# Half-row load for the last filter chunk, other TensorE fillers in the front, and a new instruction order, in a one-core H3 block with a token MLP

## The chip, the core and the metric

The kernel runs on one core of one Trainium2 chip. The metric is the device time of one execution in microseconds (us), the median of the runs that are shown; lower is better.

## The reference, cut to what matters

S = 2048 positions, D = 448 channels, F = 1792 hidden units, one batch, bf16 in and out. LN is a layer norm without weights.

```python
k_shift[s] = sum over t in 0..3 of k_pad[s + t] * shift_k[:, 3 - t]      # short causal convolution
kv = k_shift * v
y  = irfft(rfft(kv padded to 4096) * rfft(ssm_k padded to 4096))[:2048]  # long causal convolution, per channel
h  = x + LN(x) * (y + kv * ssm_D)                                        # x is A_q
z  = LN(LN(h))
out = h + transpose( gelu( z.T @ w1 + b1 ) @ w2 + b2 )                   # the MLP mixes positions, not channels
```

## The kernel before, in words

**Layout.** Position s = 16 q + r lies on partition q, in row r. Everything has 128 partitions and sixteen rows of 448 channels. The long convolution is done as a Fourier transform in two matmul stages, separately for the filter ("k1", "k2") and for kv ("u1", "u2"), then a product and two inverse stages ("i1", "i2"), then the MLP ("mlp").

**Orders written out by hand.** A step of the program is named `tag.n:m`, operation m of step n of tag. `ORDER` (L12) lists for each of the five engines every operation in the order in which that engine runs it. `_Sched.op` records each operation with what it reads and writes; `_Sched.schedule` (L322) replays the five lists to hand out the eight PSUM banks, and `emit` puts a semaphore wait ahead of each operation for what it depends on. So each engine runs its list strictly in order, and an operation that waits holds up everything behind it in its own list. DMAs are issued from the lists of SP and POOL (two from ACT).

**The front (tags dummy, loads, tables, kv, kT, k1, u1).**

- `dummy.0:1-9` (L1025) are nine matmuls of ones, 128x448, whose result nobody reads; they run while the first loads are on their way. The same matmul is used as a filler behind three of the transposing steps: `kT.1:9-11`, `kT.3:9-11`, `kT.5:9-11`, three each.
- `loads.0` to `loads.3` (L887) bring the four chunks of the filter `A_ssm_k` to KN: three of 128 channels and one of 64 channels, 4096 bytes a channel. `loads.6`, `.8`, `.10`, `.5` (L898) bring k, rows 0-3, 4-7, 8-11, 12-15; `loads.7`, `.9`, `.11`, `.12` (L901) bring v likewise. `loads.13:1` (L905) is ssm_D in 16 copies, `loads.14` (L908, L910) the two biases, `loads.4` (L890, L893) the taps.
- `kT.0` to `kT.7` (L1038) turn KN around on TensorE, chunk c and half g of the rows in step 2c + g, eight transposes each. `kT.6` and `kT.7` are the 64-channel chunk: 64x64 transposes.
- `kv.1` to `kv.8` (L966) turn k around, `kv.9` to `kv.16` (L992) are the short convolution, multiplied by v on DVE (L1007) as it leaves PSUM.
- `tables.5` and `tables.6` make the Fourier tables E (DVE L837 to L844, then a sine on ACT, L847); `tables.4` and `tables.7` make the smaller tables of the later stages (POOL, DVE, one sine on ACT, L862).
- `k1.4i+jh` and `u1.4i+jh` (L1059) are the first transform stage: eight matmuls a step, one cast of 128x896 from PSUM (L1069 on ACT or DVE; L1067 on DVE for k1.0 to k1.3), and after each second step three DMAs (two from POOL, one from SP, L1075) that shuffle the partitions. The casts go to a ring of four buffers that is released when these DMAs have landed.

**The middle.** `k2.n` and `u2.n` (L1094) are the second stage, four matmuls a step, whose casts (L738, L739 on ACT; L741, L742 on DVE) can go to either engine. Sixteen DVE products (L1160) follow, the inverse stage `i1` (L1177) with its casts (L738) and its partition shuffle (POOL L1200, SP L1200, and L1189 for the last group), and `ct` (L1108), which turns the tables around. The first product, `i1.0:0`, waits for all shuffles of k1 and u1, as its output lies over their ring. `warm` (L1210) are 14 matmuls that nobody reads. `q` and `xn` are the layer norm of x.

**The end.** `i2` (L1299, L1307) finishes the convolution row by row; for each row DVE (L1336, L1342, L1345, L1374, L1385), ACT (L1316, L1354) and POOL (L1364 to L1378) make the gated sum, its norm and the row Q[r]. `mlp.0` to `mlp.15` (L1432) multiply Q[r] with seven blocks of w1, `mlp.17` to `.23` (L1442) do the other seven, `mlp.24` to `.39` (L1454) are the second matrix with the outputs. w1 comes in eight DMAs (`w1a.0-3`, L1405, `w1b.0:0-3`, L1409), w2 in four (L1416), all from SP. `w1a.0` is needed by mlp.0.

The waits that the change touches stand in these lines:

```python
r=[(o_KN + 4096 * c, 4096), (o_ID, 256)], bw=[b], kind="tr", mode=4 if c == 3 else 0,   # kT
after=shuf["zl"] if h else shuf["u"], safter=(wl[0],) if h else ())                      # w1a.0 after all u1 shuffles
```

Of the kernel before, what the change touches and what calls it, by code (L numbers as in the profile page):

```python
# [13 lines left out]
        "dummy.0:1-9 kv.4:0-11 kv.3:0-7 kv.6:0-11 kv.5:0-7 kT.1:0-7 kT.0:0-3 kT.1:9-11 kT.0:4-7 kT.3:0-7 kT.2:0-3 "  # L14
        "kT.3:9-11 kT.5:0-7 kT.2:4-7 kT.5:9-10 kT.6:0-7 kT.7:0-7 bias.0:0 kT.5:11 kv.7:0-7 kv.2:0-3 k1.12:0-7 "
        "k1.8:0-7 k1.9:0-7 kv.2:4-11 kv.1:0-7 k1.10:0-7 k1.11:0-7 kT.4:0-7 kv.8:0-3 k1.13:0-7 k1.14:0-7 kv.8:4-11 "
        "kv.10:0-23 kv.12:0-23 kv.9:0-27 k1.4:0-7 k1.15:0-7 kv.11:0-27 u1.0:0-7 u1.1:0-7 k1.0:0-7 k1.1:0-7 u1.2:0-7 "
        "u1.3:0-7 kv.13:0-27 u1.4:0-7 k1.5:0-7 kv.14:0-23 k1.6:0-7 u1.6:0-7 u1.5:0-7 k1.2:0-7 kv.15:0-27 k1.7:0-7 "
        "u1.7:0-7 u1.8:0-7 u1.9:0-7 k1.3:0-7 k2.0:0-3 k2.1:0-3 k2.12:0-3 k2.13:0-3 k2.4:0-3 k2.5:0-3 kv.16:0-23 "
        "k2.9:0-3 k2.8:0-3 u1.10:0-7 u1.12:0-7 u1.13:0-7 u1.14:0-7 u1.11:0-7 u1.15:0-7 k2.2:0-3 k2.3:0-3 k2.7:0-3 "  # L20
        "k2.6:0-3 k2.10:0-3 k2.11:0-3 k2.14:0-3 k2.15:0-3 u2.0:0-3 u2.1:0-3 u2.12:0-3 u2.13:0-3 u2.8:0-3 u2.9:0-3 "
        "u2.6:0-3 u2.7:0-3 i1.1:1-7 i1.1:10-17 i1.1:8 i1.14:10-16 i1.14:1-7 i1.14:17 i1.14:8 i1.8:1-7 i1.8:10-16 "
        "i1.8:8 i1.8:17 ct0.0:0-7 u2.10:0-3 u2.11:0-3 i1.10:1 i1.10:10-17 i1.10:2-8 u2.5:0-3 u2.4:0-3 i1.12:1-8 "
        "i1.12:10-17 u2.3:0-3 u2.2:0-3 i1.6:1-8 i1.6:10-17 u2.14:0-3 u2.15:0-3 i1.4:9-15 i1.4:0-6 i1.4:16 i1.4:7 "
        "warm.12:0 warm.13:0 i1.16:1-7 i1.16:10-17 i1.16:8 ct.2:0-7 ct.1:0-7 ct.0:0-7 warm.0:0 warm.1:0 warm.2:0 "
        "warm.3:0 warm.4:0 warm.5:0 warm.6:0 warm.7:0 warm.8:0 warm.9:0 warm.10:0 warm.11:0 i2.1:0-1 i2.2:0-3 "
        "i2.9:0-1 i2.10:0-3 i2.17:0-1 i2.45:0-1 i2.20:0-1 i2.32:0-1 i2.28:0-1 i2.54:0 i2.41:0-1 i2.54:1 mlp.0:2 "
        "mlp.0:4 mlp.0:3 mlp.0:0 i2.58:0-1 mlp.0:6 mlp.0:5 mlp.0:1 mlp.1:6 mlp.1:1 mlp.1:3 mlp.1:5 mlp.1:0 mlp.1:4 "
        "mlp.1:2 i2.67:0-1 mlp.2:4-6 mlp.2:0-3 i2.71:0-1 mlp.3:1 mlp.3:0 mlp.3:5 mlp.3:4 mlp.3:2-3 mlp.3:6 mlp.4:2 "
        "mlp.4:1 mlp.4:6 mlp.4:5 mlp.4:4 mlp.4:0 mlp.4:3 i2.80:0-1 mlp.5:1 mlp.5:5-6 mlp.5:0 mlp.5:2 mlp.5:4 "  # L30
        "mlp.5:3 i2.84:0-1 mlp.6:1 mlp.6:6 mlp.6:0 mlp.6:3 mlp.6:5 mlp.6:4 mlp.6:2 i2.93:0-1 mlp.7:6 mlp.7:3 "
        "mlp.7:0 mlp.7:2 mlp.7:4-5 mlp.7:1 i2.97:0-1 mlp.8:2-3 mlp.8:0 mlp.8:6 mlp.8:4-5 mlp.8:1 mlp.9:0 mlp.9:3-5 "
        "mlp.9:2 mlp.9:6 mlp.9:1 mlp.10:5 mlp.10:4 mlp.10:6 mlp.10:0-1 mlp.10:3 mlp.10:2 mlp.11:3 mlp.11:6 mlp.11:2 "
        "mlp.11:0-1 mlp.11:4-5 mlp.12:2 mlp.12:0-1 mlp.12:3-6 mlp.13:2 mlp.13:1 mlp.13:0 mlp.13:3-6 mlp.14:3 "
        "mlp.14:2 mlp.14:6 mlp.14:1 mlp.14:5 mlp.14:4 mlp.14:0 mlp.15:6 mlp.15:0 mlp.15:2 mlp.15:4 mlp.15:3 "
        "mlp.15:5 mlp.15:1 mlp.17:0-15 mlp.18:0-15 mlp.19:0-15 mlp.20:0-15 mlp.21:0-15 mlp.22:0-15 mlp.23:0-15 "
        "mlp.24:0-13 mlp.25:0-13 mlp.26:0-13 mlp.27:0-13 mlp.28:0-13 mlp.29:0-13 mlp.30:0-13 mlp.31:0-13 "
        "mlp.32:0-13 mlp.33:0-13 mlp.34:0-13 mlp.35:0-13 mlp.36:0-13 mlp.37:0-13 mlp.38:0-13 mlp.39:0-10 "
        "mlp.39:16-17 mlp.39:11 mlp.39:18-20 mlp.39:12 mlp.39:21-22 mlp.39:13 mlp.39:23-29 "
    ),  # L40
    "act": (
        "tables.0:5 kv.4:12 kv.3:8 kv.6:12 tables.6:3 tables.5:3 kT.6:8 tables.7:5 k1.8:8 k1.9:8 k1.10:8 k1.11:8 "
        "k1.13:8 kT.4:8 kv.8:12 k1.15:8 k1.4:8 u1.0:8 u1.1:8 u1.2:8 u1.3:8 u1.4:8 k1.5:8 k1.6:8 u1.5:8 u1.6:8 "
        "k1.7:8 u1.8:8 u1.9:8 k2.1:4 k2.13:4-5 k2.5:5 k2.9:4 u1.12:8 u1.13:8 u1.14:8 u1.15:8 k2.3:5 k2.7:5 k2.11:4 "
        "k2.15:4 u2.1:4 u2.13:4-5 u2.9:4-5 u2.7:4-5 i1.1:18 i1.1:9 i1.14:9 i1.14:18 i1.8:9 i1.8:18 u2.11:4-5 "
        "i1.10:18 i1.10:9 u2.5:4 i1.12:9 i1.12:18 u2.3:5 u2.3:4 i1.6:9 i1.6:18 u2.15:4-5 i1.4:17 i1.4:8 xn.2:0 "
        "i1.16:18 i1.16:9 ct.2:8 xn.1:0 i1.16:21 ct.0:8 ct.1:8 xn.4:0 xn.5:0 i2.46:0 i2.19:0 i2.29:0 i2.22:0 "
        "i2.33:0 i2.42:0 i2.31:0 i2.59:0 i2.35:0 i2.44:0 i2.68:0 i2.48:0 i2.72:0 i2.57:0 i2.61:0 i2.81:0 i2.70:0 "
        "i2.85:0 i2.74:0 i2.83:0 i2.98:0 i2.87:0 i2.96:0 i2.100:0 mlp.16:6 mlp.16:2 mlp.16:0 mlp.16:4 mlp.16:3 "
        "mlp.16:5 mlp.16:1 mlp.17:16 mlp.18:16 mlp.19:16 mlp.20:16 mlp.21:16 mlp.22:16 mlp.23:16 mlp.39:15 "  # L50
    ),
    "dve": (
        "dummy.0:0 tables.3:0-1 kv.0:3 tables.6:0 tables.4:16 tables.5:0 tables.4:17 tables.6:1 tables.4:18 "
        "tables.5:1 tables.4:19 tables.6:2 tables.4:20 tables.5:2 kT.1:8 tables.7:6 kT.0:8 kT.3:8 tables.7:4 "
        "tables.7:7 kv.5:8 kT.5:8 kT.2:8 kT.7:8 bias.0:1 kv.7:8 k1.12:8 kv.2:12 kv.1:8 kv.0:4 k1.14:8 kv.10:24-25 "
        "kv.12:25 kv.12:24 kv.9:28-29 kv.11:29 kv.11:28 k1.0:8 k1.1:8 kv.13:28-29 kv.14:25 kv.14:24 k1.2:8 bias.1:0 "
        "kv.15:29 kv.15:28 u1.7:8 k1.3:8 k2.1:5 k2.5:4 kv.16:24-25 k2.9:5 u1.10:8 u1.11:8 k2.3:4 k2.7:4 k2.11:5 "
        "k2.15:5 u2.1:5 i1.0:0 i1.1:0 i1.14:0 i1.13:0 i1.7:0 i1.8:0 i1.10:0 i1.9:0 ct0.0:8 q.1:0 q.1:2 q.1:1 q.1:3 "
        "i1.11:0 i1.12:0 q.2:0 u2.5:5 i1.5:0 i1.6:0 i1.3:0 i1.2:0 q.3:0 xn.0:1 q.2:2 i1.15:0 i1.16:0 q.3:2 q.3:1 "
        "q.3:3 q.2:3 q.2:1 q.4:0 q.4:2-3 q.4:1 q.5:0 q.5:2 q.5:1 q.5:3 q.6:2 q.6:0 q.6:3 q.6:1 q.7:2 q.7:0 i2.3:0 "  # L60
        "xn.3:1 i2.4:0 i2.11:0 i2.5:0 i2.18:0 i2.6:0 i2.12:0 i2.21:0 i2.13:0 q.7:1 i2.8:0 i2.14:0 i2.55:0 i2.30:0 "
        "i2.16:0 i2.34:0 q.7:3 i2.43:0 i2.26:0 i2.27:0 i2.47:0 q.8:2 q.8:0-1 q.8:3 i2.39:0 i2.56:0 i2.60:0 i2.40:0 "
        "i2.69:0 i2.73:0 i2.52:0 i2.53:0 i2.86:0 i2.94:0 i2.65:0 i2.82:0 i2.95:0 i2.66:0 i2.78:0 i2.99:0 i2.79:0 "
        "i2.92:0 i2.91:0 i2.105:0 i2.104:0 mlp.24:14 mlp.25:14 mlp.26:14 mlp.27:14 mlp.28:14 mlp.29:14 mlp.30:14 "
        "mlp.31:14 mlp.32:14 mlp.33:14 mlp.34:14 mlp.35:14 mlp.36:14 mlp.37:14 mlp.38:14 mlp.39:14 mlp.39:30 "
    ),
    "pool": (
        "tables.4:0 tables.4:2 tables.4:4 tables.4:6 tables.4:8 tables.4:10 tables.4:12 tables.4:14 tables.4:1 "
        "tables.4:3 tables.4:5 tables.4:7 tables.4:9 tables.4:11 tables.4:13 tables.4:15 tables.1:0 tables.0:1-2 "
        "tables.0:0 tables.0:3-4 loads.13:0 tables.2:0-1 tables.2:3 tables.2:5 tables.2:7-11 tables.2:2 tables.2:4 "  # L70
        "tables.2:6 q.0:0-1 kv.0:1-2 tables.7:0-3 tables.7:8-11 kv.0:0 k1.9:9-10 k1.11:9-10 k1.13:9-10 k1.15:9-10 "
        "u1.1:9-10 u1.3:9-10 k1.1:9-10 k1.5:9-10 u1.5:9-10 k1.3:9-10 k1.7:9-10 u1.7:9-10 u1.9:9-10 u1.13:9-10 "
        "u1.15:9-10 u1.11:9-10 ew.0:3 ew.0:1 ew.0:0 i1.14:19 i1.14:21 i1.8:19 i1.8:21 i1.1:19 i1.1:21 ew.0:2 "
        "q.1:4-5 i1.10:19 i1.10:21 xn.0:0 i1.12:19 i1.12:21 i1.6:19 i1.6:21 i1.4:18 i1.4:20 q.2:4-5 q.6:4-5 xn.3:0 "
        "q.4:4-5 i2.7:0 i2.23:0-1 i2.15:0 i2.23:2 i2.24:0 i2.25:0 i2.36:0-2 i2.37:0 i2.49:0 i2.38:0 i2.49:1-2 q.8:4 "
        "i2.50:0 q.8:5 i2.51:0 i2.62:0-2 i2.63:0 i2.64:0 i2.75:0-2 i2.76:0 i2.0:0 i2.77:0 i2.88:0-2 i2.89:0 i2.90:0 "
        "i2.101:0-2 i2.102:0 i2.103:0 "
    ),
    "sp": (
        "loads.6:0 loads.8:0 loads.0:0 loads.1:0 loads.2:0 loads.3:0 loads.13:1 loads.14:0-1 loads.10:0 loads.5:0 "  # L80
        "loads.11:0 loads.4:0-2 loads.12:0 loads.9:0 loads.7:0 k1.9:11 k1.11:11 k1.13:11 k1.15:11 u1.1:11 k1.1:11 "
# [501 lines left out]
def _build(nc, A_q, A_k, A_v, A_shift_k, A_ssm_k, A_ssm_D, B_w1, B_b1, B_w2, B_b2, out):  # L583
# [54 lines left out]
    with ctx:  # L638
# [89 lines left out]
        T_KX = -27.67  # L728
        T_EW = -10.0
        T_CP, T_XL, T_WB = 39.11, -35.53, 156.06  # L730
        N_WZ, N_WI, N_W0, N_WK, N_WJ = 14, 0, 9, 3, 0

        def evac(dst, src, w, b, n, scale=None, engs=FX, r=(), est=None):

# [782 lines left out]
```

## Time and profile before

| what | value |
|---|---|
| median of the runs shown | 173.49 us (173.15 to 173.97) |
| profiled execution, its own time | 173.37 us |
| its span, first to last instruction | 171.6 us |
| around the span | 1.8 us |
| busy in the span | PE 162.5, DVE 100.9, ACT 92.6, POOL 59.4 us |
| granted TensorE clock | 1.00 in every slice |

The profile is of one execution. "Idle before" is the time in which an engine had nothing ready; a group's mean is that of one instruction, and consecutive instructions of one engine overlap by about a tenth of a microsecond, so that sums over a sequence are taken here from start to start. PE stands for matmuls, PEld for the weight loads that run beside them, and the times in the timeline are in us from the first instruction.

### The profile page before, as it was taken

The page shows a single profiled execution, that of the slowest core. Times are in us where ns is not written, and L with a number is a line of the kernel's source. Part 1 is how long each engine was busy: PE and PEld are TensorE (multiplying, and loading weights), DVE is VectorE, ACT ScalarE, POOL GpSimd, SP SyncE. Part 2 cuts the span into 40 slices and gives each one's busy share as a digit, 9 for nine tenths or more (in the row PEclk, how much of TensorE's full clock was granted, in tenths as well). Part 3 has the DMA queues.
Part 4 walks back from the last instruction along what each step waited for, and adds up shares of the span by engine and source line. Part 5 has one row for each costly group of instructions (what it writes and reads, how often), then busy time and mean ns, then how long its engine had stood idle before and what let it go on. Part 6 is the DMA issues. An engine that isn't in the chain of part 4 may idle for free.

```text
span 171.6 us, 3585 instructions
## 1 busy us (share of the span) xinstructions
PE 162.5 (95%) x1431; PEld 94.6 (55%) x1431; DVE 100.9 (59%) x187; ACT 92.6 (54%) x133; POOL 59.4 (35%) x152
## 2 busy tenths in 40 slices
PE   6989999989889999988999999999999999999994
PEld 2776745452324333533455455555567777777783
DVE  7998797879899999979997730000003133132231
ACT  3786978988999999978975816321210000000000
POOL 8345727564810696444898730000000000000000
PEclk9999999999999999999999999999999999999999
DMA  5999757676859776547989999980000111101111
GB/s 160 418 308 384 248 180 273 245 281 208 274 132 408 254 212 177 160 153 219 329 314 392 407 424 419 418 351 11 0 4 0 53 53 53 53 4 53 53 53 54
DMA packets 15628, 35.15 MB, mean 205 GB/s; under 512 B 3740, under 2 KB 9740, under 8 KB 15612
## 3 DMA queue, kind: packets, MB, share of 16 engines
q1 hardware_dynamic: 12468, 28.25, 45.3%
q0 software_dynamic: 2880, 6.49, 12.0%
q8 instruction: 11, 0.18, 0.4%
q10 hardware_dynamic: 264, 0.18, 0.3%
q14 instruction: 5, 0.04, 0.1%
HBM read 22.05 MB, written 1.84 MB: 139 GB/s over the span
## 4 chain that ended last, share of the span: by engine, by line
PE 67%; ACT 17%; DMA 7%; DVE 3%; POOL 2%; issue 2%; DVEq 0%; ACTq 0%
PE ps L1454 25%; ACT arena L738 13%; PE ps L1432 12%; PE ps L1442 12%; DMA arena<-arena 7%; PE ps L1025 3%; PE ps L1059 3%; PE ps L1094 3%; ACT arena L1069 3%; PE ps L966 3%; PE ps L1038 3%; PE ps L1299 2%; PE ps L992 2%; ACT arena L739 2%; POOL arena L1075 2%
## 5 line engine op out<-in xcount | busy, mean ns | idle before, releaser
L1457 DVE SCALAR_TENSOR_TENSOR arena<-ps,arena 128x448 bf16<-128x448 f32 (+2 forms) x17 | 11.1, 656 | 57.2 <-PE ps L1454 57.2
L1454 PE MATMUL ps<-arena 128*128 128x448 bf16 (+2 forms) x238 | 42.7, 342 | 0.0
L1454 PEld LDWEIGHTS ps<-arena 128*128 128x128 bf16 x238 | 33.3, 145 | 9.5
L738 ACT CAST arena<-ps 128x896 bf16<-128x896 f32 x30 | 24.5, 1006 | 0.3 <-PE ps L1094 0.2
L1432 PE MATMUL ps<-arena 128*128 128x448 bf16 x112 | 22.5, 353 | 0.6 <-DVE arena L1374 0.6
L1075 POOL DMA_DIRECT2D arena<-arena x32 | 17.5, 553 | 13.2 <-ACT arena L1069 9.9
L1069 ACT CAST arena<-ps 128x896 bf16<-128x896 f32 x23 | 19.5, 913 | 3.8 <-PE ps L1059 3.5
L1442 PE MATMUL ps<-arena 128*128 128x448 bf16 x112 | 21.4, 352 | 0.0
L1422 ACT ACTIVATE arena<-ps,arena 128x448 bf16<-128x448 f32 x14 | 8.2, 640 | 19.6 <-PE ps L1442 14.7
L1432 PEld LDWEIGHTS ps<-arena 128*128 128x128 bf16 x112 | 10.7, 98 | 11.3 <-DVE arena L1374 1.0
L1094 PE MATMUL ps<-arena 128*64 128x448 bf16 x128 | 15.1, 360 | 1.7 <-ACT arena L739 0.7
L1160 DVE TENSOR_TENSOR arena<-arena 128x1792 bf16<-128x1792 bf16 x16 | 16.6, 1085 | 0.3
L1442 PEld LDWEIGHTS ps<-arena 128*128 128x128 bf16 x112 | 11.0, 98 | 10.2
L1177 PE MATMUL ps<-arena 64*128 64x448 bf16 x128 | 14.7, 351 | 1.1 <-DVE arena L1160 0.7
L1059 PE MATMUL ps<-arena 128*32 128x448 bf16 x256 | 15.2, 355 | 0.5
L1200 POOL DMA_DIRECT2D arena<-arena x14 | 8.3, 596 | 13.2 <-ACT arena L738 13.2
L1094 PEld LDWEIGHTS ps<-arena 128*64 128x64 f16 x128 | 5.7, 108 | 10.3 <-ACT arena L738 3.2
L1177 PEld LDWEIGHTS ps<-arena 64*128 64x128 f16 x128 | 5.9, 94 | 9.7 <-DVE arena L1160 3.2
L738 ACT COPY arena<-ps 128x1024 bf16<-128x1024 bf16 (+2 forms) x9 | 8.3, 977 | 3.3 <-PE ps L966 2.8
L1007 DVE TENSOR_TENSOR arena<-ps,arena 128x512 bf16<-128x512 f32 (+1 forms) x16 | 9.0, 616 | 1.4 <-PE ps L992 1.4
L1354 ACT ACTIVATE arena<-arena 128x448 bf16<-128x448 f32 x14 | 8.0, 573 | 3.0 <-DVE arena L1326 2.9
L1059 PEld LDWEIGHTS ps<-arena 128*32 128x32 f16 x256 | 5.0, 95 | 7.9 <-ACT arena L1069 2.4
(96 smaller groups left out, 195.5 us busy)
## 6 DMA issues: line engine op xcount, KB each, us to landing
arena<-in_B_w_dram SPq DMA_DIRECT2D x8, 896.0 KB, 7.8
arena<-in_B_w_dram SPq DMA_DIRECT2D x2, 2048.0 KB, 17.6
arena<-arena SPq DMA_DIRECT2D x16, 224.0 KB, 3.0
arena<-arena POOLq DMA_DIRECT2D x32, 112.0 KB, 3.5
arena<-in_B_w_dram SPq DMA_DIRECT2D x2, 1536.0 KB, 20.1
arena<-arena POOLq DMA_DIRECT2D x14, 196.0 KB, 4.7
arena<-in_A_k_dram SPq DMA_DIRECT2D x4, 448.0 KB, 5.5
arena<-in_A_v_dram SPq DMA_DIRECT2D x4, 448.0 KB, 8.7
```

The source lines that it names most:

```text
L738: return e.copy(out=dst(), in_=src())
L1007: return e.tensor_tensor(out=v, in0=u.rearrange("p t (r d) -> p t r d", d=64), in1=v, op=ALU.mult)
L1059: op("pe", lambda e, W, b=b, r=r, q=q, x=x, c0=c0: e.matmul(PS[32 * q:32 * q + 32, b.slots[x], 0:D], E[:, 2 * r + x, c0:c0 + 32], src[:, r ...
L1069: return e.copy(out=dst, in_=Ppair(b)) if W == "act" else e.tensor_copy(out=dst, in_=Ppair(b))
L1075: shuf[tag].append(op(q_, lambda e, W, g=g, i=i, a=a, nu=nu, jh=jh: e.dma_start(T[a + i:a + i + 4 * nu - 3:4].rearrange("p (j k) c d -> p ...
L1094: op("pe", lambda e, W, b=bs[h], h=h, j=j, c=c, par=par: e.matmul(PS[64 * par:64 * par + 64, b.slots[c], 0:D], FW[:, 64 * c:64 * c + 64], ...
L1160: op("dve", lambda e, W, m=m, i=i: e.tensor_tensor(out=MR(m.slots[0]).rearrange("p (x y) d -> p x y d", x=2), in0=TU[:, i].unsqueeze(2).br ...
L1177: k = op("pe", lambda e, W, b=bs[h], m=ms[h], par=par, t=t, tab=tab, xy=xy, P=P: e.matmul(Pb(b, par), tab[P, :], MR(m.slots[0])[P, xy, :], ...
L1432: op("pe", lambda e, W, r=r, fc=fc, b=bs[fc]: e.matmul(Pb(b), W1A[:, r, 128 * fc:128 * fc + 128], Q[:, r, :], start=(r == 0), stop=(r == R ...
L1442: op("pe", lambda e, W, r=r, fc=fc, b=b: e.matmul(Pb(b), W1B[:, r, 128 * (fc - n0):128 * (fc - n0) + 128], Q[:, r, :], start=(r == 0), sto ...
L1454: op("pe", lambda e, W, r=r, fc=fc, b=b, d0=d0, d1=d1: e.matmul(Pb(b)[:, d0:d1], W2[fc // 7][:, fc % 7, r:S:R], G[:, fc, d0:d1], start=(fc ...
L1457: op("dve", lambda e, W, r=r, b=b, A=A, d0=d0, d1=d1: e.scalar_tensor_tensor(out=X[:, r, d0:d1], in0=Pb(b)[:, d0:d1], scalar=bm[:, r:r + 1 ...
```

## The change

**Loads and transposes of the last filter chunk.** The 64 channels of 4096 bytes are loaded as 128 half channels of 2048 bytes. `kT.6` and `kT.7` are no longer eight transposes of 64x64 each but sixteen matmuls each: 128 half rows against the even or the odd columns of the identity, 64 columns wide, the two halves into the lower and the upper 64 partitions of one PSUM bank, in f32.

**Fillers.** A new tag `fill` puts five matmuls like the dummies ahead of the nine. Behind the kT steps one filler is left (`kT.1:9`) of nine.

**w1a.0** waits for one inverse shuffle (`i1.8:21`) instead of all u1 shuffles.

**ORDER** is another one on all engines. The parts that the prediction uses are below; in words: on SP k rows 4-7, filter chunks 0 and 2 come first, then k rows 0-3, chunks 3 and 1; ssm_D, the second bias and v rows 8-11 go behind two shuffle issues; w1a.0 goes behind the i1.16 shuffles, and w1a.1 to w1a.3 are spread between the late i1 shuffles. On POOL `tables.7` goes from before the first shuffles to between them. On DVE `tables.5` goes ahead, `tables.4` behind the transposes. ACT no longer copies kv.4 and kv.6.

```diff
 "pe"
-dummy.0:1-9 kv.4:0-11 kv.3:0-7 kv.6:0-11 kv.5:0-7 kT.1:0-7 kT.0:0-3 kT.1:9-11 kT.0:4-7 kT.3:0-7 kT.2:0-3
-kT.3:9-11 kT.5:0-7 kT.2:4-7 kT.5:9-10 kT.6:0-7 kT.7:0-7 bias.0:0 kT.5:11 kv.7:0-7 kv.2:0-3 k1.12:0-7
...
-i2.1:0-1 i2.2:0-3 i2.9:0-1 i2.10:0-3 i2.17:0-1 i2.45:0-1 i2.20:0-1 i2.32:0-1 i2.28:0-1 i2.54:0 i2.41:0-1 i2.54:1 mlp.0:2
-mlp.0:4 mlp.0:3 mlp.0:0 i2.58:0-1 mlp.0:6 mlp.0:5 mlp.0:1 ...
+fill.0:0 fill.2:0 fill.4:0 fill.3:0 fill.1:0 dummy.0:1-9 kv.6:0-3 kv.5:0-7 kT.1:0-7 kT.1:9 kT.0:0-7
+kv.6:4-11 bias.0:0 kT.5:0-7 kv.3:0-6 kv.4:0-11 kT.6:0-15 kT.7:0-15 kv.3:7 kT.3:0-7 kT.2:0-7 kv.7:0-7
+k1.8:0-7 k1.12:0-7 k1.9:0-7 kv.2:0-3 kv.1:0-7 ...
+i2.1:0-1 i2.2:0-3 i2.9:0-1 i2.10:0-3 i2.45:0-1 i2.32:0-1 i2.17:0-1 i2.20:0-1
+i2.28:0-1 warm.0:0 i2.54:0-1 i2.41:0-1 i2.58:0-1 mlp.0:3 mlp.0:6 mlp.0:1 mlp.0:4 mlp.0:2 mlp.0:5 mlp.0:0
 "act"
-... u1.9:8 k2.1:4 k2.13:4-5 k2.5:5 k2.9:4 u1.12:8 u1.13:8 u1.14:8 u1.15:8 k2.3:5 k2.7:5 k2.11:4 k2.15:4 u2.1:4
+... u1.4:8 tables.7:5 k1.5:8 ... k2.1:4 k2.13:4 k2.5:5 k2.9:4 u1.12:8 u1.13:8 u1.14:8 u1.15:8 k2.3:5 k2.7:5 k2.11:4 k2.15:4 u2.13:5
 "dve"
-... i2.3:0 xn.3:1 i2.4:0 i2.11:0 i2.5:0 i2.18:0 i2.6:0 i2.12:0 i2.21:0 i2.13:0 q.7:1 i2.8:0 i2.14:0 i2.55:0
+... i2.3:0 xn.3:1 i2.4:0 i2.11:0 i2.5:0 i2.12:0 i2.6:0 i2.13:0 i2.18:0 i2.14:0 i2.21:0 i2.55:0 i2.8:0
 "sp"
-loads.6:0 loads.8:0 loads.0:0 loads.1:0 loads.2:0 loads.3:0 loads.13:1 loads.14:0-1 loads.10:0 loads.5:0 loads.11:0 ...
+loads.8:0 loads.0:0 loads.2:0 loads.14:0 loads.6:0 loads.3:0 loads.1:0 loads.10:0 loads.5:0 loads.4:2 loads.4:0-1
+loads.12:0 loads.9:0 loads.7:0 k1.13:11 k1.11:11 loads.14:1 loads.13:1 k1.9:11 loads.11:0 ...
...
-N_WZ, N_WI, N_W0, N_WK, N_WJ = 14, 0, 9, 3, 0
+N_WZ, N_WI, N_W0, N_WK, N_WJ = 14, 0, 9, 1, 0
...
+            op(Dq, lambda e, W: e.dma_start(
+                KN[:, 3, 0:S // 2], A_ssm_k[384:448, :].rearrange("c (h s) -> (c h) s", h=2)),
+               w=[(o_KN + 4096 * 3, 2048)], dmab=128 * 2048)
...
+        def emit_fill():
+            for i in range(5):
+                b = _Buf(psum)
+                sch.t0 = -50.0 + i
+                op("pe", lambda e, W, b=b: e.matmul(Pb(b), DUM[:, 0:128], DUM, start=True, stop=True),
+                   r=[(o_DUM, DB)], bw=[b], n=D)
...
+                        for h in range(2):
+                            k = op("pe", lambda e, W, b=b, rr=rr, r=8 * g + rr, h=h: e.matmul(
+                                PS[64 * h:64 * h + 64, b.slots[0], 64 * rr:64 * rr + 64], KN[:, 3, r:S // 2:R],
+                                ID[:, h:128:2], start=True, stop=True),
...
-                if i < 3:
+                if i < 1:
                     dummy(N_WK, T_KT + 1.0 * (2 * i + 1), (k,))
...
-                       after=shuf["zl"] if h else shuf["u"], safter=(wl[0],) if h else ())
+                       after=shuf["zl"] if h else [shuf["zpool7"]], safter=(wl[0],) if h else ())
```

## The prediction

> **What bounds the kernel now.** I read the page first (busy time by slice, then the chain that ended last), then that chain in order of time, then the timelines of single engines around its joints.
>
> The page, section 2 and the chain by engine:
>
> ```profile
> PE   6989999989889999988999999999999999999994
> ...
> PEclk9999999999999999999999999999999999999999
> ...
> PE 67%; ACT 17%; DMA 7%; DVE 3%; POOL 2%; issue 2%; DVEq 0%; ACTq 0%
> ```
>
> TensorE is busy and its clock full throughout, so only its few waits, and work on it that nobody needs, can be won. The chain in order of time (start, length, what) tells where it waits:
>
> ```profile
> 1.38 3.23 PE ps L1025 x9
> ...
> 30.74 3.90 DMA arena<-arena
> ...
> 34.73 0.96 PE ps L1094 x8
> ...
> 47.55 13.62 ACT arena L738 x17
> ...
> 71.20 4.38 DMA arena<-arena
> ...
> 75.63 0.55 PE ps L1299 x2
> ...
> 81.39 0.92 PE ps L1432 x4
> ```
>
> The joints: k2.0 starts at 34.73 when the shuffle of k1.5 has landed; the casts of u2 start on ACT at 47.5 and run without a break to i1.4, the last of them ending at 70.33; the shuffle of i1.4 lands at 75.58; the first Q row is ready at 81.32 and mlp.0 starts at 81.38. From there 87 us of matmuls follow with no wait, so the change is worth what it does to that last number, plus matmuls that it takes out behind it.
>
> **The front, to k2.0.** The timeline of PE:
>
> ```profile
> 4.45 2.40 PE L966 MATMUL ps<-arena 128*128 128x128 bf16 x40
> 6.78 0.96 PE L1038 MATMUL ps<-arena 128*128 128x128 bf16 x12
> 7.58 0.73 PE L1025 MATMUL ps<-arena 128*128 128x448 bf16 x3
> 8.14 0.42 PE L1038 MATMUL ps<-arena 128*128 128x128 bf16 x4
> ```
>
> The nine dummies took 3.23 us, 0.36 each, against 0.19 for the same shape at full clock (mlp, 1.32 for seven). Five more at full clock are 0.95 us, so the first transposes start at 5.4 for 4.45. That costs nothing as long as the next wait ends later, and it does: kv.3 needs the bank that kT.1:8 on DVE frees, behind the tables. DVE starts that copy at 8.35 now; with tables.5 ahead of the identity I get 7.97 (1.6 for POOL's iotas, 0.67 for the three small steps, 5.70 for the table rows without tables.4), so the bank is free at 8.7. Before that PE has 3.2 us of transposes and one filler, which fit from 5.4. If the cold stretch were to last 1 us longer, this cover would just be used up.
>
> Loads: they move 410 GB/s; k rows land at 4.38 and 5.48, filter chunks at 6.73, 7.97, 9.94, 11.20. The last two were late, for the small packets of ssm_D and the biases lie there (9.0 to 10.5: 270 GB/s over the window 8 to 11). The new sequence without them, 1.1 us for 0.46 MB and 1.25 for 0.52 MB from 4.38: 5.6 (chunk 0), 6.9 (chunk 2), 8.2 (k rows 0-3), 8.8 (chunk 3; its halved rows in 0.64, where it took 1.26), 10.1 (chunk 1), 11.2 (k rows 8-11; 12.2 now). All are there before their place in PE's list comes up. The b2, ssm_D and v loads sent behind two shuffles (to about 20 on SP) are needed by k1.0 at 24.2 and by kv.13 at 27: they land 3.4 to 4.5 us after issue, so ssm_D just fits.
>
> Eight fillers less are 8 x 0.19 = 1.5 us. kT.6 and kT.7: 16 small transposes took 1.1 us (0.07 each). The trace has no 64-column matmul of this form; the nearest rows are the half transposes of kv.2 (0.35 for eight, 0.044 each) and the convolution matmuls of kv.10 (0.68 for 24, 0.028 each). 32 of them cost 0.9 to 2.2 us; I take 0.044 x 32 = 1.4, as these have the same 64-column weights. The Trainium skill, page "TensorE: Matmul & The Clock Gate", section "LDWEIGHTS (loading the stationary operand)", gives 53 ns for 64 columns: 1.7 us by that estimate, and the sum 0.3 us worse; the strided 128-column loads in this trace took 75 ns each (3.6 us for 48).
>
> Step by step with these (0.46 for eight transposes, 0.5 strided, 0.1 when the array is divided anew): kv.3 8.7, kv.4 9.1 (its bank waits for the bias copy behind a 1.9 us sine on ACT), kT.6 9.9, kT.7 10.6, kT.3 11.4, kT.2 11.9, kv.7 12.4, k1.8 at 13.0. Now the first k1 step starts at 13.86. Of that 0.9 us little survives: DVE multiplies kv by v one engine behind, and u1.0 starts now at 23.26, when kv.9 ends at 23.21. In the new order kv.12 can start at 18.9 on PE, DVE at 19.7 for 20.06, and u1.0 at 22.9. But k1.15 now stands ahead of the convolution, so its shuffles are issued near 20 and not at 23.58, the ring buffer for u1.4 is free in time (ACT waits 0.67 us for it at 28.20 now), and POOL makes the tables.7 (3.1 us) in the gap 20.85 to 23.58 where it idles now. The sine of tables.7 costs ACT 0.6 us here. I get k1.5 off ACT at 29.1 (29.91), its POOL issues at 29.15 to 30.2 (30.20 to 31.28), landing 3.9 us after the second at 33.6; PE is through its own list at 33.5. k2.0 at 33.7: **1.0 us earlier**.
>
> **k2 to i1.** One cast of k2.13 goes from ACT to DVE. ACT's casts are 0.80 us apart, DVE's 1.0; between 34 and 48 ACT is busy 12.6 us of 14, DVE 12.1. Banks go back and forth between the two, so I book no more than 0.2: the first u2 cast at 46.3 (47.54). The first product i1.0 waits for u2.1:4, which is now second on ACT: 48.1 for 48.84. From there the lists hold the same sums: 28 casts on ACT to i1.4, and on DVE 15 products and the same statistics bar one of 0.6 ahead of the last product. Between the lead of 0.75 on DVE and 1.25 on ACT I take **1.0** at the end of i1.4; the landing takes its 4.38 again (4.0 to 5.2 for most of that line's issues), and i2.1 starts at 74.6.
>
> **i2 and mlp.** DVE is in an unbroken run here:
>
> ```profile
> 76.97 0.68 DVE L1336 SCALAR_TENSOR_TENSOR arena<-ps,arena 128x448 f32<-128x448 f32 x1 [1.05 <-PE ps L1307]
> ...
> 80.84 0.48 DVE L1385 TENSOR_SCALAR arena<-arena 128x448 bf16<-128x448 f32 x1
> 81.23 0.15 DVE L1374 TENSOR_SCALAR arena<-arena 128x1 f32<-128x1 f32 x1
> 81.30 0.68 DVE L1318 TENSOR_SCALAR arena<-ps,arena 128x448 f32<-128x448 f32 x1
> ```
>
> 3.87 us lie between the first row's i2.3 and the i2.8 that gives Q[0]. The new list has i2.14 and i2.55 ahead of i2.8 as well and q.7:1 behind it: 0.07 + 0.60 - 0.07, so **0.6 later**. In turn i2.58 is done ahead of mlp.0, hidden behind i2.8, and not within it: **0.38 less** behind. Q[1] to Q[4] keep their distance (Q[2] needs 3.97 us from the end of i2.21 now, and has 4.2).
>
> w1a.0 is issued behind i1.16 on SP, at about 73.2, not at 49.70. It is queued behind three shuffle issues and ahead of small ones for rows 14 and 15 that nobody needs before mlp.7. Like w1a.1 it takes 4.9 us and lands at 78.1, and mlp.0 wants it at 81.0. Hidden by 2.9 us; at the 8.1 that w1a.3 took, by nothing.
>
> Sum: 173.37 (the profiled execution) - 1.0 + 0.6 - 0.38 = **172.6**. The profiled execution is 0.12 below the median; I leave the forecast at 172.6. Less than about 0.9 us (0.5%) either way can hardly be told from no change, and the boundary, 172.62, lies on this forecast.
>
> **Rivals.** (1) The clock. The longest stretch with transposes alone is now 4.61 to 7.58, 3.0 us; then come fillers. In the new order it is 6.8 to 9.9, and to 13.0 if the narrow matmuls of kT.6 count for little. The profile shows full clock, but never with so few ordinary matmuls. If the clock falls there, at least one stretch like the first one is paid: nine dummies took 3.23 for 1.7 us at full clock, 1.5 us; with the casts behind it 1.8, all on PE's path to k2.0: 172.6 + 1.8 = 174.4, slower. It decides where ordinary matmuls are more than some 3 us apart. The Trainium skill, same page, section "Part 4: PE-mode transpose", says that transposes do not count as TensorE activity in the same way; by that rule the clock falls. This trace neither confirms nor excludes it.
>
> (2) DVE keeps the front where it is: u1.0's lead of 0.4 is all that reaches k2.0, since DVE's list from kv.12 on has the same products and 0.75 us of tables.7 more. For it: DVE is 8.0 of 10 us busy from 24 to 34, with gaps only for PE. Then 173.37 - 0.4 + 0.6 - 0.38 = 173.2, no change. The same comes out if w1a.0 lands late by 0.6.
>
> (3) More is won: DVE's lead grows as on ACT (k2.13 moved, i1.16 by 1.3 earlier) and i2.1 starts 1.9 earlier: 171.7.
>
> That the edits are not what they say, I exclude: the lists are run as written.
>
> **How the numbers follow.** Forecast 0.54, its own range 172.1 to 173.2 (kT.6 from 0.9 to 2.2, the lead at i1.4 from 0.75 to 1.25): 0.38 faster by over 0.5%, 0.16 within. Clock 0.22: 0.20 slower, 0.02 within. DVE 0.16: 0.14 within, 0.02 slower. More won 0.08, faster. Sums: faster 0.46, same 0.32, slower 0.22. The range 171.7 to 174.4 takes in the ends of the cases; leaving out half of (1) and of (3) above and below is some 0.15.
>
> **What would show it.** Right: granted clock 1.00 between 5 and 14; first k1 matmul near 13.0, k2.0 near 33.7, first u2 cast near 46.3, i2.1 near 74.6, 4.5 us from i2.3 to i2.8, mlp.0 near 81.0 with no wait for w1a.0. Wrong: matmuls of 128x448 at 0.36 us behind the front (rival 1), DVE ending the waits of u1 and k2 (rival 2), or PE idle before mlp.0 until a w1 DMA lands.

## The result and the profile after

The changed kernel takes **175.69 us** (median of six executions, 175.0 to 177.83) beside 173.29 for the kernel before in the same session (six, 173.15 to 173.97): **1.0122 times the time, interval 1.0094 to 1.0150**, slower. A ratio leaves out executions more than 1.5% above the fastest of their kernel; a median has them all. The profiled execution took 176.0 us, its span 174.2.

The page, section 2, and the chain by engine, after:

```profile
PE   6999996999899999979899999999999999999994
...
PEclk9999999999999999999999999999999999999999
...
PE 72%; ACT 12%; DVE 5%; DMA 5%; SPq 2%; issue 1%; POOL 1%; DVEq 0%
```

The clock row still shows full clock everywhere, and the first 24 matmuls of k1 took 1.32 us as before, so the clock did not fall behind the transposes of this execution. New in the chain is **SPq, 2%**: time in which SP does nothing but issue DMAs. The chain in order of time shows where:

```profile
17.21 2.56 ACT arena L1090 x3
19.79 0.65 SPq L1096
...
20.48 0.73 SPq L1096
...
21.25 0.93 SPq L917
...
22.22 0.81 SPq L912
...
23.07 4.60 DMA arena<-arena
...
27.76 1.10 DVE arena L1088
...
77.88 0.55 PE ps L1320 x2
...
129.22 42.08 PE ps L1475 x231
```

In the kernel before, SP issued the shuffle of k1.9 at 16.67, and k1.0's cast on DVE began at 24.85 (the second row holds two casts):

```profile
16.67 0.64 SPq L1075 DMA_DIRECT2D arena<-arena  x1
...
24.85 2.09 DVE L1067 TENSOR_TENSOR arena<-ps,arena 128x896 bf16<-128x896 f32 x2 [0.15 <-PE ps L1059]
```

Read the chain after from its end. k1.0 on DVE (L1088) starts at 27.76, after DVE has been idle for 2.03 us. It was released by a shuffle DMA that SP issued at 23.07: the SP shuffle of **k1.9**, which landed at 27.68. Ahead of it SP issued the shuffles of k1.13 (at 19.79, when its cast was done) and k1.11, then bias 2 (L917) and ssm_D (L912), 0.65 to 0.93 us each. k1.9 was ready at 17, but stood behind k1.13 in SP's list. Why k1.0 has to wait for it: k1.8 to k1.11 share one of the four ring buffers, k1.0 to k1.3 write the same one, and it is free only when all six shuffles of k1.9 and k1.11 have landed. ssm_D, which k1.0 reads, landed at 27.13, barely sooner: 4.9 us after its issue at 22.22.

The marks, from start to start, beside those of before (the last forecast is worked out from the others):

| mark (us) | before | predicted | after |
|---|---|---|---|
| first transposes on PE | 4.45 | 5.4 | 6.58 |
| first k1 matmul | 13.86 | 13.0 | 14.49 |
| u1.0 | 23.26 | 22.9 | 24.59 |
| k1.0 on DVE | 24.85 | 24.2 | 27.76 |
| k2.0 | 34.73 | 33.7 | 36.88 |
| i1.0 on DVE | 48.84 | 48.1 | 51.63 |
| i2.1 | 75.63 | 74.6 | 77.88 |
| mlp.0 | 81.38 | 81.0 | 84.36 |
| mlp.24 | 126.41 | 125.7 | 129.05 |

From k2.0 to the end the forecast holds within 0.1 us at i2.1 and mlp.0 (41.0 us from k2.0 to i2.1 for 40.9 forecast, 6.48 from there to mlp.0 for 6.4). Nearly the whole miss, 3.2 of the 3.4 us at mlp.0, lies ahead of k2.0.

### The profile page after: what moved, and what is told of

It reads as the page before. It is cut to its first block, busy times and chain, and to the rows that moved or that the text cites. A ratio compares the mean times of both kernels' runs of the same rounds, so it can differ in the third digit from the quotient of the medians.

```text
span 174.2 us, 3620 instructions
## 1 busy us (share of the span) xinstructions
PE 164.3 (94%) x1444; PEld 95.6 (55%) x1444; DVE 102.8 (59%) x188; ACT 91.1 (52%) x132; POOL 58.7 (34%) x152
## 3 DMA queue, kind: packets, MB, share of 16 engines
q0 software_dynamic: 2880, 6.49, 11.6%
## 4 chain that ended last, share of the span: by engine, by line
PE 72%; ACT 12%; DVE 5%; DMA 5%; SPq 2%; issue 1%; POOL 1%; DVEq 0%
PE ps L1475 24%; PE ps L1453 12%; PE ps L1463 12%; ACT arena L741 7%; DMA arena<-arena 5%; PE ps L1198 5%; PE ps L1080 4%; ACT arena L1090 3%; PE ps L1115 3%; PE ps L1032 2%; PE ps L973 2%; PE ps L1320 2%; PE ps L999 2%; ACT arena L742 2%; PE ps L1053 2%; PE ps L1039 1%
## 5 line engine op out<-in xcount | busy, mean ns | idle before, releaser
L741 ACT CAST arena<-ps 128x896 bf16<-128x896 f32 (+2 forms) x33 | 25.8, 1000 | 1.2 <-PE ps L1058 0.8
L1090 ACT CAST arena<-ps 128x896 bf16<-128x896 f32 x24 | 20.4, 912 | 5.1 <-PE ps L1080 4.0
L1453 PE MATMUL ps<-arena 128*128 128x448 bf16 x112 | 22.4, 353 | 0.0
L1463 PE MATMUL ps<-arena 128*128 128x448 bf16 x112 | 21.4, 353 | 0.0
L1453 PEld LDWEIGHTS ps<-arena 128*128 128x128 bf16 x112 | 10.8, 98 | 10.5 <-DVE arena L1406 0.6
L1320 PE MATMUL ps<-arena 128*128 128x448 bf16 x32 | 7.9, 353 | 1.7 <-DMA arena<-arena 1.0
L1406 DVE TENSOR_SCALAR arena<-arena 128x448 bf16<-128x448 f32 x16 | 7.6, 507 | 3.1 <-POOL arena L1399 3.1
```

The costliest lines, as they stand in the source:

```text
L741: return e.copy(out=dst(), in_=src())
L1090: return e.copy(out=dst, in_=Ppair(b)) if W == "act" else e.tensor_copy(out=dst, in_=Ppair(b))
L1320: k = op("pe", lambda e, W, b=b, r=r, h=h: e.matmul(Pb(b), ET[:, 2 * r + h, :], TZ[:, r, h, :], start=(h == 0), stop=(h == 1 and r >= NZ)) ...
L1453: op("pe", lambda e, W, r=r, fc=fc, b=bs[fc]: e.matmul(Pb(b), W1A[:, r, 128 * fc:128 * fc + 128], Q[:, r, :], start=(r == 0), stop=(r == R ...
L1463: op("pe", lambda e, W, r=r, fc=fc, b=b: e.matmul(Pb(b), W1B[:, r, 128 * (fc - n0):128 * (fc - n0) + 128], Q[:, r, :], start=(r == 0), sto ...
```

## The experiments

Theory 1: the loss is SP's queue, which holds up k1.0. Theory 2: it is PE's front, cold fillers and dear transposes. Sessions differ (the kernel before had medians of 173.9 to 174.1 in the later ones), so kernels are compared by their ratios to it. Kernels named a_ start from the changed kernel, those named b_ from the kernel before.

| kernel | median us | ratio to before, interval |
|---|---|---|
| changed kernel | 175.69 | 1.0122 (1.0094 to 1.0150) |
| a_ring: k1.9's shuffle first | 175.47 | 1.0081 (1.0052 to 1.0110) |
| a_sp: SP's queue mended | 174.59 | 1.0040 (1.0021 to 1.0058) |
| a_tr: and last chunk as before | 174.02 | 1.0018 (0.9982 to 1.0055) |
| a_tr_i2: and i2 nearly as before | 175.67 | 1.0080 (1.0049 to 1.0110) |
| a_nofill: changed, no five fillers | 175.58 | 1.0101 (1.0069 to 1.0134) |
| b_sp: before, SP's piece alone | 176.71 | 1.0120 (1.0083 to 1.0156) |
| b_half: before, half rows alone | 174.81 | 1.0050 (1.0028 to 1.0072) |
| b_fill: before, five fillers alone | 174.32 | 1.0025 (0.9996 to 1.0055) |
| b_tail: before, lists from i2 on alone | 174.55 | 1.0029 (1.0002 to 1.0056) |
| b_mid: before, lists u2.9 to i2 alone | 174.53 | 1.0032 (1.0002 to 1.0063) |
| b_nk: before, no fillers at kT | 173.49 | 0.9975 (0.9945 to 1.0005) |
| b_late: before, ssm_D behind the v loads | 174.28 | 0.9994 (0.9961 to 1.0027) |

The pieces put alone into the kernel before (b_sp, b_half, b_fill, b_tail, b_mid, b_nk) add up to 2.3%, and the whole change costs 1.22%: the price of a piece alone is not its share of the loss.

**SP's queue, undone in two steps.** First the ring buffer's shuffle alone (a_ring), on SP:

```diff
-loads.7:0 k1.13:11 k1.11:11 loads.14:1 loads.13:1 k1.9:11 loads.11:0
+loads.7:0 k1.9:11 k1.13:11 k1.11:11 loads.14:1 loads.13:1 loads.11:0
```

Expected:

> The changed kernel with one edit: on SP the shuffle of k1.9 goes ahead of that of k1.13 again, not behind it, k1.11 and two loads. In the changed kernel k1.0 on DVE waits until 27.76; the k1.9 shuffle, which releases the ring buffer that k1.0 writes, lands at 27.68, and ssm_D, which k1.0 reads, at 27.13. Theory 1 (SP's queue, both of these): the ring is free early, ssm_D still lands near 27.1, so k1.0 starts near 27.2, k2.0 near 36.4 for 36.88, about 175.2. Theory 1a (the ring buffer alone): k1.0 at 25.8, k2.0 near 35.2, 174.0. Theory 2 (the loss is PE's front alone, cold fillers and dear transposes): no change, 175.7.

k1.0 started at 27.20, k2.0 at 36.32: as theory 1 has it, the next wait is ssm_D. Then both (a_sp):

```diff
-loads.4:0-1 loads.12:0 loads.9:0 loads.7:0 k1.13:11 k1.11:11 loads.14:1 loads.13:1 k1.9:11 loads.11:0
+loads.4:0-1 loads.14:1 loads.13:1 loads.12:0 loads.9:0 loads.7:0 k1.9:11 k1.11:11 k1.13:11 loads.11:0
```

> The changed kernel with SP's queue mended: bias 2 and ssm_D are issued ahead of the v loads again, and the shuffles of k1.9, k1.11, k1.13 in the order in which they come ready. Theory 1: k1.0 on DVE starts right behind kv.11 at 25.8, u1.4 no longer waits for the shuffle of k1.15, k2.0 near 35.2 (36.88), time 174.0 (173.7 to 174.5), still slower than before by what PE's front and the i2 order cost. Theory 2: the lists of PE, ACT and DVE are full anyway, k2.0 at 36.4 or later, 175.2 or more.

k1.0 came at 25.56, k2.0 at 35.48, and the ratio fell from 1.0122 to 1.0040; the time, 174.59, lies between those of the two theories. **About two thirds of the loss, 0.8% or 1.4 us, is the order of SP's queue here** (by the two intervals, 0.5 to 1.2%). The chain of a_sp no longer has SP in it between 16.8 and 36 us. Not all of the 1.4 us by which k2.0 came earlier in this profile is SP's: the first k1 matmul came 0.44 earlier too, with a clock that rose at 5.5 us and not at 6.9. From u1.0 to k2.0 it took 11.34 us for 12.29.

The gain of 1.0 us that was forecast at k2.0 did not come back with it: 35.48 is still later than the 34.73 of before. k2.0 waits, as before, for the last POOL shuffle of k1.5, which was issued at 31.52, for 30.74 before:

```profile
31.52 3.87 DMA arena<-arena
...
35.48 0.96 PE ps L1115 x8
```

**SP's piece alone, put into the kernel before** (b_sp):

```diff
-loads.3:0 loads.13:1 loads.14:0-1 loads.10:0 ... loads.7:0 k1.9:11 k1.11:11 k1.13:11 k1.15:11
+loads.3:0 loads.14:0 loads.10:0 ... loads.7:0 k1.13:11 k1.11:11 loads.14:1 loads.13:1 k1.9:11 loads.11:0 k1.15:11
```

> The kernel before with the changed kernel's piece of SP's queue alone: bias 2, ssm_D and v rows 8-11 behind the shuffles of k1.13 and k1.11, the shuffle of k1.9 behind ssm_D. Theory 1: the shuffle of k1.9 leaves SP near 22.6 and lands near 27, so k1.0 on DVE starts near 27.0 for 24.85, k2.0 1.0 to 1.4 us later than in the kernel before, time +1.0 to +1.4. Theory 2 (the order of SP costs little, the front does): +0.3 at most.

The ratio is 1.0120, 2.1 us, more than expected. Its chain repeats the picture of the changed kernel:

```profile
19.57 0.64 SPq L1075
...
23.37 4.12 DMA arena<-arena
...
27.57 1.10 DVE arena L1067
```

ssm_D had landed at 24.87 here, 2.7 us before k1.0 started; k1.9's shuffle landed at 27.49. So the ring buffer is what decides, and ssm_D only the next in line. This profile is of the execution of 178.10 us, with a mean clock of 0.99, and shows a second thing, the clock. The stretches around the wait (stretch and length, busy time of PE, PEld, DVE, ACT, POOL, clock, DMA share, GB/s):

```profile
24.00:26.00 2.00, 1.88 (x40) 0.47 (x31) 0.90 (x2) 1.93 (x3) 0.86 (x2) 1.00 0.75 182
26.00:28.00 2.00, 0.54 (x8) 0.10 (x8) 0.43 (x1) 1.71 (x2) 1.08 (x2) 1.00 0.89 305
28.00:30.00 2.00, 1.28 (x22) 1.14 (x24) 1.66 (x2) 0.00 (x0) 1.13 (x3) 0.57 0.93 366
30.00:32.00 2.00, 2.00 (x30) 0.88 (x26) 1.29 (x2) 0.40 (x1) 1.02 (x2) 0.58 0.67 255
```

PE stood still from 26.54 to 28.71, and its clock was 0.57 and 0.58 in the two stretches from 28 to 32 us: kv.13 took 1.89 us for 1.06. In 7 of 12 executions of b_sp the mean clock was 0.99 or less, at 176.49 to 179.56 us. But the other five took 174.32 to 176.77, 175.9 in the mean, 2.0 more than the kernel before: most of the price is there without the low clock, and why it is above the 1.0 to 1.4 expected stays open. The wait of 1.3 us on PE in the changed kernel's profile did not do this, but one of its six executions, the one of 177.83, had 0.99; of 102 executions of the kernel before that ran beside the experiments, one did.

**The half rows alone, in the kernel before** (b_half): the load and the `kT.6`/`kT.7` code of the change, and in the lists

```diff
-kT.6:0-7 kT.7:0-7
+kT.6:0-15 kT.7:0-15
```

and the same for the copies behind them.

> The kernel before with one part of the change: the last filter chunk as 128 half rows, kT.6 and kT.7 as 16 matmuls each; order, fillers and loads' sequence as before. Theory 2: the 32 matmuls take 2.0 us where the 16 transposes took 1.1, the load lands 0.6 earlier and helps nobody, the first k1 matmul is near 14.8 (13.86), k2.0 near 35.3 and the time 173.8 to 174.3. Theory 1: PE's front has cover, no change: 173.3.

First k1 matmul at 14.79, k2.0 at 35.41, ratio 1.0050, 0.9 us: as theory 2 has it. The 16 transposes before, and the 32 matmuls in their place in b_half:

```profile
11.68 1.18 PE L1038 MATMUL ps<-arena 64*128 64x64 bf16 x16
...
11.66 2.13 PE L1048 MATMUL ps<-arena 128*64 128x64 bf16 x32
```

With the changed order the runs do not settle the price: taking the half rows out of a_sp (a_tr: the load, the code and these list entries as in the kernel before) brought 1.0040 to 1.0018, and the two intervals overlap.

> The changed kernel with SP's queue mended (as in the run of that edit alone, 174.59) and, besides, the last filter chunk as before: 64 rows of 4096 bytes, kT.6 and kT.7 as eight 64x64 transposes each. Theory 2: 0.9 us less on PE in the front reach k1.8 (13.1 for 14.05) and k2.0 (34.6 for 35.48): 173.7. If PE's front has cover there, no change: 174.6.

In a_tr's profile the k1 steps started 0.60 us earlier than in a_sp's, but k2.0 only 0.16. So the gain in the front is mostly absorbed by k2.0, and a_tr can't be told from the kernel before. Its first k1 matmul came at 13.45, earlier than the 13.86 of before, but k2.0 at 35.32, later than the 34.73. Why the 32 small matmuls are dear, the weight loads after, by shape, 4 to 15 us (busy us, mean ns, idle before):

```profile
L1053 PEld LDWEIGHTS ps<-arena 128*128 128x128 bf16 x40 | 2.9, 148 | 0.1
L1058 PEld LDWEIGHTS ps<-arena 128*64 128x64 bf16 x32 | 2.0, 217 | 0.0
L973 PEld LDWEIGHTS ps<-arena 128*64 128x64 bf16 x16 | 0.5, 109 | 0.2
```

L1058 is kT.6 and kT.7 with 64 columns picked at a stride of 16; L1053 the other kT steps with 128 columns at that stride; L973 half transposes with 64 columns in a row. From start to start a pair of kT.6 took 0.120, 0.060 each, and the strided 128-column ones 0.062 each: with a stride, half the columns saved nothing. That the stride of the weights is the reason is not shown by itself, for kT.6 and kT.7 also read every second column of the identity. The Trainium skill, page "TensorE: Matmul & The Clock Gate", section "LDWEIGHTS (loading the stationary operand)", counts columns, 53 ns for 64; these rows do not halve so.

**The fillers.** In the changed kernel all fourteen matmuls ahead of the transposes ran at 0.37 us:

```profile
1.38 2.05 PE L1039 MATMUL ps<-arena 128*128 128x448 bf16 x5 [1.38 <-DVE arena L1024]
3.22 3.57 PE L1032 MATMUL ps<-arena 128*128 128x448 bf16 x9
6.58 1.00 PE L973 MATMUL ps<-arena 128*128 128x128 bf16 x12
```

The five fillers taken out of the changed kernel (a_nofill):

```diff
-fill.0:0 fill.2:0 fill.4:0 fill.3:0 fill.1:0 dummy.0:1-9
+dummy.0:1-9
```

> The changed kernel without the five fillers ahead of the nine dummies. Theory 2: the first transposes start at about 4.6 and not at 6.58; DVE's tables keep kT.1's copy at 8.65, so about 0.6 of it reaches k1.8 (13.9 for 14.49); k2.0 near 36.3, 175.1. Theory 1: it is all SP's queue; as that hangs on the cast of k1.13, at most the same 0.6 moves, and if the fillers were hidden nothing does: 175.1 to 175.7. Also read here: when the matmuls go from 0.37 to 0.19 us. If a number of matmuls decides, the ninth dummy as before (4.1 us); if a clock of its own decides, anywhere between 3 and 7 us.

The transposes began at 4.71, 1.9 us earlier, but those up to 6.0 came at 0.107 us each and not at 0.056; the k1 steps began 0.44 earlier, and the ratio, 1.0101, can't be told from 1.0122. Two of its six executions (176.47 and 176.64 us) had a mean clock of 0.99. Put into the kernel before (b_fill, the reverse edit):

> The kernel before with the five fillers ahead of the nine dummies, nothing else. By the prediction (0.19 us each, PE waits 0.7 for DVE's tables at 9.09): +0.2 at most. By what the profile after showed (0.37 us each as long as the clock is low, which was until 4.1 to 7.5 in the runs so far): the first transposes at 5.4 to 6.6 for 4.45, kT.1's copy 0.2 to 1.2 later, time +0.3 to +1.0, and more spread between executions.

kT.1's copy came at 8.77 for 8.35, k2.0 at 35.07; 1.0025, not clearly above 1. So the fillers cost 0.55% at most.

**No fillers at kT, in the kernel before** (b_nk; `kT.1:9-11`, `kT.3:9-11` and `kT.5:9-11` left out):

> The kernel before without the nine fillers behind the kT steps; from 4.45 to 13 us TensorE has transposes alone. If transposes do not hold the clock (rival 1 of the prediction), matmuls of 448 columns come at 0.37 us for a stretch after about 8 and the time is 1.5 to 2 us more. If they do: three of the nine stand where PE waits for DVE anyway, six cost 1.1 us; k1.12 near 12.9 for 13.86, of which DVE lets 0.3 to 0.8 reach k2.0: 0.3 to 0.8 us less than before.

Neither case came as described. In the profiled execution the clock rose at about 6.3, in the midst of transposes alone, and stayed up through 7.5 us of them; and k1.12 came at 13.81 for 13.86. Of the 1.7 us that the nine fillers take, 0.8 went to the clock, which rose 2.1 us later than in the profile before (kT.1 at 7.60 for 6.78), and PE waited 0.91 (0.21 for ACT's copy, 0.35 for a load, 0.35 for DVE's copy), where it waited 0.52 before. The ratio, 0.9975, allows for a gain of up to 1.0 us or none. But in three of its twelve executions the mean clock was 0.981 to 0.990, at 175.67 to 177.16 us, where the others took 173.02 to 174.47. The Trainium skill, same page, section "Part 4: PE-mode transpose", has the full clock not engaging for transposes; this trace disagrees for the execution that it shows. That the three slower ones lost it in the transposes is likely, but no trace of one was taken.

**The tail** (b_tail: PE, ACT, DVE and POOL of the change from i2 on):

> The kernel before with the changed kernel's lists of PE, ACT, DVE and POOL from i2 on (SP's as before). By the sum of the prediction, as the profile after bears it out (i2.1 to mlp.0 6.5 us for 5.75, 0.35 less behind mlp.0): +0.4 us. If the rows behind the first one gain by the new order: no change.

1.0029, 0.5 us: i2.1 to mlp.0 6.49 us, 0.34 less behind mlp.0. The attempt to mend it in the changed order (a_tr_i2) failed:

```diff
-i2.18:0 i2.14:0 i2.21:0 i2.55:0 i2.8:0 i2.16:0
+i2.18:0 i2.21:0 i2.8:0 i2.14:0 i2.55:0 i2.16:0
...
-i2.41:0-1 i2.58:0-1 mlp.0:3 mlp.0:6 mlp.0:1 mlp.0:4
+i2.41:0-1 mlp.0:3 mlp.0:6 mlp.0:1 mlp.0:4 i2.58:0-1
```

> The kernel of the run before this one, and i2 nearly as before: on DVE i2.8 ahead of i2.14 and i2.55, on PE i2.58 behind four matmuls of mlp.0. By the sum of the prediction: mlp.0 0.7 earlier after i2.1 (5.8 us for 6.5), 0.38 more behind it, together 0.3 less: 173.4. If Q[0] is not what mlp.0 waits for: no change or 0.4 more.

mlp.0 came 5.84 us after i2.1, as expected, but behind it 1.6 us were lost, not 0.4: mlp.2 waited 0.9 us for Q[2] (i2.26 on DVE ended at 87.23, behind POOL's i2.25), and its profiled execution also began later. Only part of before's order was put back, and not POOL's, on which Q[2] hangs.

**The middle** (b_mid: PE, ACT, DVE and POOL of the change between u2.9 or i1.0 and i2):

> The kernel before with the changed kernel's lists from u2.9 and i1.0 up to i2 alone (the products, inverse stage, statistics; u2.1 first on ACT as before). In the profile after this stretch, i1.0 on DVE to i2.1 on PE, took 26.25 us for 26.79: 0.5 us less, 173.5 where the kernel before has 173.95. If the stretch was shorter only because it began later (transfers of the stage before were out of the way), no change.

The stretch took 26.90 us, not 26.25: the 0.5 us of the changed kernel were no merit of this order, at least not alone. A later beginning is not the reason either: in a_sp and a_tr the stretch began at 50.15 and 49.99 (49.87 in b_mid) and took 26.27 and 26.38. SP's order in this stage, with w1a.0 at its end, was not tried; b_mid has that of the kernel before.

**ssm_D late but not too late** (b_late), an attempt at a version that beats both:

```diff
-loads.3:0 loads.13:1 loads.14:0-1 ... loads.7:0 k1.9:11
+loads.3:0 loads.14:0 ... loads.7:0 loads.14:1 loads.13:1 k1.9:11
```

> The kernel before with ssm_D and bias 2 issued behind the v loads and ahead of the first shuffle, nothing else. In the profile before, filter chunk 2 lands 1.97 us behind chunk 1 (1.24 between chunks 0 and 1), with the small packets of these loads beside it; in two profiles of the same front (the kernels with the changed tail and the changed middle) it landed at 11.44 and 10.99, kT.5 started at that moment, and k1.12 came at 15.04 and 14.76 for 13.86. If ssm_D's packets take that bandwidth: chunk 2 near 9.3 to 10.3, ssm_D near 20, in time for k1.0 at 24.85, and 0.3 to 0.8 us less than before in the median, with less spread. If chunk 2 is late for another reason: no change.

No clear change, 0.9994: chunk 2 still landed at 10.16, 1.85 behind chunk 1, without ssm_D beside it. No version that beats the kernel before was found.

## Why the prediction was wrong

- **The step that failed** is the one in the front on SP: "its shuffles are issued near 20 and not at 23.58, the ring buffer for u1.4 is free in time" and "ssm_D just fits". I followed k1.15's ring buffer and ssm_D, and not k1.9's, whose SP shuffle I never placed. It stood fifth in a row whose first, the shuffle of k1.13, waits for an ACT cast that ends at 19.77; with 0.65 to 0.93 us for each of the four issues ahead of it and 4.60 to land, k1.0's buffer is free at 27.7, where k1.0 was due at 24.2. What I did follow was late too: ssm_D landed at 27.13, and SP's shuffle of k1.15 left at 24.29, not near 20 (23.32 before). Undone, the order gives back about 1.4 us; alone it costs the kernel before 2.1. I even named the general case, a late landing, under rival 2, but for w1a.0 and 0.6 us.
- **The gain of 1.0 us at k2.0** came in no run. With SP's queue mended k2.0 was still 1.8 us behind the forecast: 1.05 of it is the first k1 matmul (14.05 for 13.0), and from u1.0 to k2.0 it took 11.34 us, for 10.8 forecast and 11.47 before. I let k1.5's POOL issues follow its cast at 29.15; in a_sp the last of them began at 31.52, behind those of u1.3 and k1.1. What holds that part of the front beside this was not tried.
- **kT.6 and kT.7: the term was mis-sized.** I took 0.044 for each of 32 matmuls and 1.4 us; it was 2.0. The right row was that of the strided transposes (0.062 from start to start, 0.07 in my own working for the old kT.6), not the half transposes, whose columns lie in a row.
- **The fillers: mis-sized, and of little weight.** I took 0.95 us for five; they took 0.37 each, all fourteen, and the transposes started at 6.58 for 5.4. The clock's rise has a time of its own, not that of the ninth dummy. I had said that the cover is used up if the cold stretch lasts 1 us longer; it lasted 2.8 longer, kT.6 began 1.0 late (10.88 for 9.9), and with 0.6 for the 32 matmuls that makes the 1.5 us at the first k1 matmul.
- **Eight fillers less as 1.5 us** was too much: without all nine the kernel before gained 0.4 us in the ratio, 1.0 at most, and 0.05 at the first k1 matmul of the profile, where waits and a later clock took their place.
- **Right:** i2 (0.6 more forecast, 0.73 measured; 0.38 less behind mlp.0, 0.34 measured), and that w1a.0 is hidden: it landed at 82.76, 1.6 before mlp.0, though it took 6.2 us from its issue and not 4.9.
- **Right by luck:** the distance from k2.0 to i2.1. From k2.0 to i1.0 it took 14.75 us for 14.4 forecast (14.11 before), so the gain booked for the moved cast did not come, and from i1.0 to i2.1 26.25 for 26.5. The landings of the loads came within 0.2 us of the forecast, but the reason that I gave for the late chunks, the small packets of ssm_D and the biases, did not hold for ssm_D: without it beside them chunk 2 was 1.85 us behind chunk 1 in b_late and 2.25 in b_sp.
- **The rivals.** None of the three is the cause of the loss in this profile. The clock rival had the right sign only: the clock was low for the first 5.5 us of matmuls, but did not fall in the transposes of this execution. One of the six executions had a mean clock of 0.99; where it was low there was not traced. Rival 2, that DVE keeps k2.0 where it is, was hidden by SP's wait and is not excluded for what is left: in a_tr the chain to k2.0 runs over DVE's products of kv and v (2.55 us from 20.95, 1.91 from 30.19).

## What to carry to other kernels

Where an engine issues DMAs in a written order, place every issue in time: one that waits for a late producer holds up all behind it, and a small shuffle behind it can hold a buffer that the next stage writes. For each buffer of a ring ask which of its readers ends last, on which queue. A load that is moved from an idle stretch of a queue to behind a waiting one is not hidden by the time that its consumer had before.

## What was not expected of the hardware

- **When the clock becomes full is not set by the kernel.** In the 14 profiles here the matmuls went from 0.373 to 0.19 us (or transposes from 0.107 to 0.056) between 4.2 and 7.1 us, with the first matmul at 1.37 or 1.38 in all of them: 4.2 before, 6.9 after, 6.0 without the five fillers, 5.0 in b_fill, 6.3 in b_nk. The kernel before and b_late have the same list on PE, and the clock rose at 4.2 in the one and near 7.1 in the other. The clock row shows 1.00 in this time all the same; only the spacing tells. The Trainium skill, page "TensorE: Matmul & The Clock Gate", section "What's actually happening", tells of a window of 3.4 us that runs freely. These times, 2.8 to 5.7 us after the first matmul, spread over 2.9 us, which fits into one such window; the same part's 500 ns from run to run does not agree with them.
- **The front of the kernel before varies with its loads.** Filter chunk 2 landed at 9.94 in the profile before, but at 11.44 in b_tail, where PE then waited for it:

```profile
11.48 0.96 PE L1039 MATMUL ps<-arena 128*128 128x128 bf16 x12 [0.76 <-DMA arena<-in_A_ssm_k_dram]
```

  That put k1.12 at 15.04 for 13.86 in the same front. The kernel before took 173.02 to 176.29 us over its 102 executions beside the experiments. Why the landing varies stayed open (in b_late it landed at 10.16 without ssm_D beside it).
